# Moving the block sums of h to the head of a unit on GpSimd, tying ScalarE's copies of them to later matmuls, and making weight-block sums in three stages, in a fused attention and gated-MLP kernel

## The chip, the cores and the metric

The kernel runs on one core of a Trainium2 chip. Its time is the device time of one execution in microseconds (us); a set of runs is given by its median. In a profile the engines are PE (TensorE's matmuls; PEld is its weight loads), ACT (ScalarE), DVE (VectorE), POOL (GpSimd) and SP (SyncE, which here only issues DMA transfers). Each engine takes its own instructions in a fixed order and waits, one instruction at a time, for semaphores of the others.

## The reference, cut to what matters

All tensors are float32; S = 2048 rows, D = 576 columns, 32 heads of 18, F = 4608.

```python
x  = A_x
xn = layernorm(x)
q, k, v = split_heads(xn @ A_wqkv)            # 32 heads
s  = (softmax(q @ k.T * 18**-0.5) @ v) @ A_wo
gate, up = xn @ B_W_gate, xn @ B_W_up
h  = gate * (gate > 0) * up                   # 2048 x 4608
g  = silu(h @ B_W_down)
out = x + s * g
```

The matrix products are made with operands split into a high and a low part (float32r), three products for one: high by high, high by low, low by high.

## The kernel before

**Units.** After the layer norm and the QKV products the work runs in 144 units, numbered k = 0 to 143: four groups of 512 rows (g) times 36 blocks of 128 features of F (f). A unit is 27 steps of the up product (`pg`: 9 chunks of the contraction, three products each). Each step issues two matmuls, one on each half of TensorE's rows. Into these steps attention is dealt: up to 8 score matmuls per half for the row maxima of the next pair of heads (`pm`, reduced by VectorE, `mx`, L269), and from unit 16 on 8 per half for the exponentials of the present pair (`psx`, ScalarE's `p`, L97). So a unit in the middle of the run has 43 steps, 16 reductions and 16 exponentials. Both kinds of score, and the down product's results (`py`), use the same five PSUM banks in turn (`psS`).

**After its steps** a unit makes h: ScalarE takes the gate through Relu (`h<-pg`), VectorE multiplies by up (L739). An odd unit then runs the matmuls of P by V (`po`); an even one runs the down product of the two units before it (`py`). So a pair of units is, in PE's order: odd unit's steps, `po`, even unit's steps, `py`.

**The down product** is plain for the first 36 units. From unit 36 on two blocks of h are combined with two blocks of W_down in 7 products in place of 8: it needs sums of quarters of h1 and h2, the blocks of an even and the following odd unit (`first_half`, `second_half`), and the matching sums of weight blocks, which units 1 to 35 make and store in DRAM (`wtd`; `make_items`, `make_step`). Each sum of h is made by GpSimd into a scratch tile (`hr`, in a single buffer of tag `e`), copied by ScalarE as its high part (`ha`, `hb`, `hd`, `hc`), and GpSimd subtracts the copy for the low part (`low`). The results of the 7 products are added up by VectorE and, by way of ScalarE's copies (`add`, L879), by GpSimd (`c`, `y`).

**What sets the order.** PE, GpSimd and VectorE take their instructions in the order in which the code issues them, and so does SP until unit 17. ScalarE's are placed by a scheduler unless they are pinned. `up_end` puts the functions that make the sums into `at_step`, keyed by the step of the next unit at which they run. In a unit GpSimd's program begins with `split_up(k + 1)`, which makes the high and low parts of the next unit's up weights (`gw<-rg`, a cast and a subtraction), then the rows of `run_later` (`nr`), then what the steps issue. In the odd units of the last pair of heads `out_weights` loads and splits a block of wo, ahead of the steps.

**Group ends.** When f is 35 the sums of the group are combined (`combine`, 8 additions for each of two halves), and a gate (`gate_step`: Tanh on ScalarE, two GpSimd operations, a store) runs at two steps of each of the next units. The x tiles of the next group of rows are loaded in the last unit of a group (`load_x`).

**Weight blocks.** `make_step` runs three times in most units below 16 and five times in a unit from 16 to 35. Each time it ends the item before (GpSimd's subtraction `ws`, the store to `wtd`) and starts the next: a sum `wt` on VectorE (below unit 16) or GpSimd, and ScalarE's copy `ws` (L965). Tiles `wt` and `ws` have two buffers each.

Of the kernel before, what the change touches and what calls it, by code (L numbers as in the profile page):

```python
# [12 lines left out]
ALU = mybir.AluOpType  # L13
# [6 lines left out]
def kernel(  # L20
# [43 lines left out]
    def pool(stack, name, bufs, side="left", **kw):  # L64
        return stack.enter_context(tc.tile_pool(name=name, bufs=bufs, side=side, reuse_waits="tile", **kw))

    def mm(*args, **kw):
        return tc.keep_in_program_order(nc.tensor.matmul(*args, **kw))  # L68

# [696 lines left out]
    def low(t, cs, raw):  # L766
        gp.tensor_tensor(t[:, 1, cs], raw, t[:, 0, cs].bitcast(F32), ALU.subtract)

    def first_half(h):

        s, z = slice(0, 256), slice(256, 512)
        st = {}

        def raws():
            a = st["a"] = hp.tile([P, 2, 512], F32R, tag="hh", name="ha", bufs=3)
            r = st["r"] = wl.tile([P, D], F32, tag="e", name="hr", bufs=1)
            nc.scalar.activation(a[:, 0, s], h[:, s], AF.Copy)
            gp.tensor_tensor(r[:, s], h[:, z], h[:, s], ALU.subtract)
            nc.scalar.activation(a[:, 0, z], r[:, s], AF.Copy)

        def lows():
            a, r = st["a"], st["r"]
            low(a, s, h[:, s])
            low(a, z, r[:, s])
            hops[2] = a, 0
            hops[5] = a, 2

        return {2: [raws], 8: [lows]}

    def second_half(hs):  # L790

        h1, h2 = hs
        s, z = slice(0, 256), slice(256, 512)
        st = {}

        def raws():
            b = st["b"] = hp.tile([P, 2, 512], F32R, tag="hh", name="hb", bufs=3)
            d = st["d"] = mw[0].tile([P, 2, 256], F32R, name="hd", bufs=1)
            r = st["r"] = wl.tile([P, D], F32, tag="e", name="hr", bufs=1)
            nc.scalar.activation(b[:, 0, z], h2[:, z], AF.Copy)  # L800
            gp.tensor_tensor(r[:, s], h2[:, s], h2[:, z], ALU.subtract)
            nc.scalar.activation(b[:, 0, s], r[:, s], AF.Copy)
            gp.tensor_tensor(r[:, z], h1[:, s], h2[:, z], ALU.add)
            nc.scalar.activation(d[:, 0], r[:, z], AF.Copy)

        def lows():
            b, d, r = st["b"], st["d"], st["r"]
            low(b, z, h2[:, z])
            low(b, s, r[:, s])
            low(d, s, r[:, z])  # L810
            hops[6] = b, 0
            hops[3] = b, 2
            hops[0] = d, 0
            c = st["c"] = hp.tile([P, 2, 512], F32R, tag="hh", name="hc", bufs=3)
            r = st["r"] = wl.tile([P, D], F32, tag="e", name="hr", bufs=1)
            gp.tensor_tensor(r[:, :512], h1, h2, ALU.add)
            nc.scalar.activation(c[:, 0], r[:, :512], AF.Copy)

        def rest():
            c, r = st["c"], st["r"]  # L820
            low(c, slice(0, 512), r[:, :512])
            hops[4] = c, 0
            hops[1] = c, 2

        return {2: [raws], 8: [lows], 13: [rest]}

# [17 lines left out]
    def down_made(k):  # L844
# [94 lines left out]
    def make_items(fp):  # L939
# [9 lines left out]
        def start(m, on):  # L949
# [7 lines left out]
            if op is not None:  # L957
# [5 lines left out]
                x0 = t  # L963
            s_ = pw.tile([P, 2, HC], F32R, name="ws")
            nc.scalar.activation(s_[:, 0], x0, AF.Copy)  # L965
            st[m] = x0, s_

# [4 lines left out]

        return [(load, start, end, m) for m in (None, 1, 4, 0, 2, 3, 5, 6)]

    for fp in range(NF // 2):
        items.extend(make_items(fp))
    open_items = []

    def make_step(on):
        while open_items:  # L980
            end, m = open_items.pop()
            end(m)
        if items:
            load, start, end, m = items.pop(0)
            if m is None:
                load()
            else:
                start(m, on)
                open_items.append((end, m))

# [53 lines left out]
    def gate_step(spill_=True):  # L1044
        if gates:
            y, t = gates.pop(0)
            e = wl.tile([P, D], F32, name="e", bufs=1)
            tc.keep_in_program_order(nc.scalar.activation(e, y, AF.Tanh, scale=0.5))
            gp.tensor_scalar(e, e, 0.5, 0.5, op0=ALU.mult, op1=ALU.add)
# [124 lines left out]

    def emit_unit(k, ex, ns, mx, nm):
        if k - 1 in rds:
            split_down(k - 1)
        steps = dict(at_step)
        at_step.clear()
        if k not in rds and k not in dws and k != NF - 1:  # L1180
# [9 lines left out]
        if k % 2:  # L1190
            if k in rds:
                split_down(k)
            for _ in range(2):
                if to_load:
                    out_weights(to_load.pop(0))
        n = KC * len(PRODUCTS) + ns + nm
# [204 lines left out]
```

## Time and profile before

| | |
|---|---|
| median of 3 runs | 3601.24 us (3600.57 to 3614.94) |
| the profiled execution | 3614.0 us |
| its span, first to last instruction | 3612.2 us |
| mean granted TensorE clock | 0.876 |
| busy: PE, PEld, DVE, ACT, POOL | 81%, 59%, 53%, 47%, 48% |

Times in the views are us from the span's start. A row of the timeline gives start, duration, engine, line, operation, tiles written and read, shape and count, and in brackets how long the engine sat idle before it and what ended that. A row of the waits says who waited for whom: us in total, times, longest. A row of the windows gives a stretch, its length, each engine's busy time (with the number of instructions), the granted TensorE clock (1.00 is full), the share of time for which the 16 DMA engines were busy, and GB/s. L68 and L85 are helpers through which all matmuls and all GpSimd instructions pass.

### The profile page before, as it was taken

The numbers are of one execution on the slowest core, as the hardware profiler recorded it, in microseconds if no ns is written. First come the engines' busy times: TensorE is split into PE (matmuls) and PEld (weight loads), VectorE is DVE, ScalarE is ACT, GpSimd is POOL, SyncE is SP. The second block draws the span as 40 slices with busy tenths as digits, with TensorE's granted clock in tenths as the row PEclk, the third lists the DMA queues.
The fourth block names the chain that finished last, engine by engine and source line by source line (L and its number), as shares of the span: only waits on it lengthen the run. The fifth ranks groups of instructions, "written<-read, shape, count | busy, mean of one in ns | idle before, by whom it ended". The sixth has DMA issues, their size and how long they took to land.

```text
span 3612.2 us, 63126 instructions
## 1 busy us (share of the span) xinstructions
PE 2920.0 (81%) x24653; PEld 2138.8 (59%) x24653; DVE 1898.3 (53%) x3118; ACT 1710.9 (47%) x3761; POOL 1737.2 (48%) x1762
## 2 busy tenths in 40 slices
PE   9957778777747888989855998888882889888789
PEld 8846665555435666666633666666652566666558
DVE  5234444555425666666633766666661666666215
ACT  3211124444424655555523655565552565566553
POOL 4235554555425444554424455445532645544556
PEclk9978888888868989998976999899985999999899
DMA  8543443433314332333313333333322333332227
GB/s 273 183 145 113 125 121 94 119 118 96 118 64 125 88 93 82 91 92 105 88 63 95 94 86 97 101 93 88 94 74 85 110 90 91 93 86 75 81 85 221
DMA packets 324977, 382.12 MB, mean 106 GB/s; under 512 B 33480, under 2 KB 214472, under 8 KB 324680
## 3 DMA queue, kind: packets, MB, share of 16 engines
q1 hardware_dynamic: 316936, 350.43, 33.3%
q0 software_dynamic: 7744, 27.66, 2.2%
q8 instruction: 195, 3.19, 0.4%
q14 instruction: 102, 0.84, 0.1%
HBM read 293.78 MB, written 83.69 MB: 104 GB/s over the span
## 4 chain that ended last, share of the span: by engine, by line
PE 31%; POOL 31%; DMA 9%; ACT 5%; issue 4%; SPq 1%; DVE 0%; ACTq 0%; POOLq 0%; DVEq 0%
PE pg L68 15%; POOL gw L85 12%; PE psx L68 6%; PE pm L68 5%; POOL hr L85 5%; POOL y L85 4%; POOL c L85 4%; DMA x<-xTd 3%; PE py L68 3%; ACT p L97 2%; DMA rg<-in_B_W_up_dram 2%; POOL hb L85 2%; PE pw L68 1%; SPq L97 1%; DMA wtd<-ws 1%
## 5 line engine op out<-in xcount | busy, mean ns | idle before, releaser
L269 DVE TENSOR_REDUCE mx<-pm 128x1 f32<-128x512 f32 x2048 | 1370.0, 689 | 1126.1 <-PE pm L68 923.4
L68 PE MATMUL pg<-x,gw 64*128 64x512 f32 x7533 | 1624.8, 439 | 86.4 <-DMA x<-xTd 72.7
L68 PEld LDWEIGHTS pg<-x,gw 64*128 64x128 f32 x7533 | 1135.5, 212 | 238.3 <-DMA x<-xTd 79.3
L97 ACT ACTIVATE p<-psx 128x512 f32<-128x512 f32 x2048 | 1098.3, 601 | 227.4 <-PE psx L68 163.6
L85 POOL CAST gw<-rg 128x1152 fp32r<-128x1152 f32 x131 | 151.1, 1153 | 659.1 <-PE pg L68 436.7
L68 PE MATMUL po<-p,va 128*32 128x512 f32 x4096 | 456.8, 598 | 0.0
L85 POOL TENSOR_TENSOR c<-add,c 128x288 f32<-128x288 f32 x204 | 157.9, 807 | 584.3 <-ACT add L879 584.3
L68 PE MATMUL psx<-qT,kq 56*128 56x512 f32 x608 | 263.7, 446 | 129.9 <-ACT p L97 129.9
L85 POOL TENSOR_TENSOR gw<-rg,gw 128x1152 fp32r<-128x1152 f32 x131 | 346.0, 2641 | 10.6
L68 PEld LDWEIGHTS po<-p,va 128*32 128x32 f32 x4096 | 126.7, 110 | 296.1 <-issue 285.2
L68 PE MATMUL psx<-kq,kA 56*128 56x512 f32 x512 | 224.5, 450 | 88.9 <-ACT p L97 88.9
L68 PE MATMUL psx<-kq 56*128 56x512 f32 x512 | 227.7, 459 | 84.4 <-ACT p L97 84.4
L68 PE MATMUL psx<-qT,kA 56*128 56x512 f32 x416 | 185.8, 461 | 119.3 <-ACT p L97 119.3
L68 PE MATMUL pm<-kq,qT 54*128 54x512 f32 x608 | 260.4, 453 | 17.8 <-ACT p L97 17.8
L68 PE MATMUL pm<-kq 54*128 54x512 f32 x512 | 213.8, 440 | 37.9 <-ACT p L97 24.3
L68 PE MATMUL pm<-kA,kq 54*128 54x512 f32 x512 | 220.2, 455 | 28.8 <-DMA kA<-kd 19.0
L68 PEld LDWEIGHTS psx<-qT,kq 56*128 56x128 f32 x608 | 128.4, 211 | 161.4 <-ACT p L97 146.2
L68 PE MATMUL pm<-kA,qT 54*128 54x512 f32 x416 | 172.1, 436 | 23.9 <-ACT p L97 23.9
L739 DVE TENSOR_TENSOR h<-pg,h 128x512 f32<-128x512 f32 x144 | 98.3, 683 | 159.5 <-ACT h L97 107.6
L965 ACT ACTIVATE ws<-wt 128x288 fp32r<-128x288 f32 x90 | 39.8, 443 | 298.6 <-DMA wtd<-ws 158.5
L68 PEld LDWEIGHTS psx<-kq 56*128 56x128 f32 x512 | 110.9, 217 | 114.7 <-ACT p L97 101.8
L68 PEld LDWEIGHTS psx<-kq,kA 56*128 56x128 f32 x512 | 109.0, 213 | 116.8 <-ACT p L97 104.1
(138 smaller groups left out, 4490.0 us busy)
## 6 DMA issues: line engine op xcount, KB each, us to landing
w<-wtd SPq DMA_DIRECT2D x378, 288.0 KB
rg<-in_B_W_gate_dram SPq DMA_DIRECT2D x131, 288.0 KB
rg<-in_B_W_up_dram SPq DMA_DIRECT2D x131, 288.0 KB
wtd<-ws SPq DMA_DIRECT2D x126, 288.0 KB
x<-xTd SPq DMA_DIRECT2D x36, 512.0 KB
rd<-in_B_W_down_dram SPq DMA_DIRECT2D x36, 288.0 KB
wp<-in_B_W_down_dram SPq DMA_DIRECT2D x36, 288.0 KB
qd<-hh POOLq DMA_DIRECT2D x16, 512.0 KB, 6.8
```

Source lines behind the costliest of these rows:

```text
L68: return tc.keep_in_program_order(nc.tensor.matmul(*args, **kw))
L85: return lambda *args, **kw: tc.keep_in_program_order(op(*args, **kw))
L97: i = op(*args, **kw)
L269: vec(nc.vector.tensor_reduce(mx[:, h, b, j, c : c + 1], ps, axis=AX.X, op=ALU.max))
L739: vec(nc.vector.tensor_tensor(h, ps[1], h, ALU.mult))
L965: nc.scalar.activation(s_[:, 0], x0, AF.Copy)
```

## The change

1. **Sums first.** The GpSimd sums of h (`raws`) run under key 0, at the very head of a unit, ahead of `split_up`; the sum of all of h1 and h2, made at step 8 before, joins them and is written over h1.
2. **Copies tied.** ScalarE's copies of the sums go through `copy_now`, which makes a copy wait for the newest matmul issued: in an odd unit at steps 11 and 13, in an even one at 7, 14, 15 and 17. The low parts move from steps 8 and 13 to 22, 23 and 27.
3. **Group ends.** `combine` runs whole at the head of a unit, behind the sums, where it ran at steps 11 and 21. Gates run at steps 24 and 33 (17 and 27 before), their Tanh tied to the newest matmul. `out_weights` runs at steps 25 and 29 of an odd unit, no longer at its head.
4. **Three stages.** `make_step` subtracts and stores the item started two calls ago, copies the one started at the last call (tied), and starts a new one without its copy.

The core of the diff:

```diff
+    def copy_now(dst, src):
+        after(nc.scalar.activation(dst, src, AF.Copy), newest[0])
...
-        return {2: [raws], 8: [lows]}
+        return {
+            0: [raws],
+            11: [lambda: copy_now(st["a"][:, 0, s], h[:, s])],
+            13: [lambda: copy_now(st["a"][:, 0, z], st["r"][:, s])],
+            22: [lows],
+        }
...
             gp.tensor_tensor(r[:, s], h2[:, s], h2[:, z], ALU.subtract)
-            nc.scalar.activation(b[:, 0, s], r[:, s], AF.Copy)
             gp.tensor_tensor(r[:, z], h1[:, s], h2[:, z], ALU.add)
-            nc.scalar.activation(d[:, 0], r[:, z], AF.Copy)
+            gp.tensor_tensor(h1, h1, h2, ALU.add)
...
-        return {2: [raws], 8: [lows], 13: [rest]}
+        return {
+            0: [raws],
+            7: [lambda: copy_now(st["b"][:, 0, z], h2[:, z])],
+            14: [lambda: copy_now(st["b"][:, 0, s], st["r"][:, s])],
+            15: [lambda: copy_now(st["d"][:, 0], st["r"][:, z])],
+            17: [lambda: copy_now(st["c"][:, 0], h1)],
+            23: [lows], 27: [rest],
+        }
...
-                at_step[11] = [lambda: run_tasks(todo[:1])]
-                at_step[21] = [lambda: run_tasks(todo[1:])]
+                at_step.setdefault(0, []).extend((lambda j=j: combine(j)) for j in range(2))
...
     def make_step(on):
-        while open_items:
-            end, m = open_items.pop()
-            end(m)
+        ended = open_items.pop(0)
+        if ended:
+            ended[1](ended[2])
+        if open_items[0]:
+            open_items[0][0](open_items[0][2])
+        open_items.append(None)
...
     def emit_unit(k, ex, ns, mx, nm):
+        steps = dict(at_step)
+        at_step.clear()
+        for fn in steps.pop(0, ()):
+            fn()
...
-            if i in (17, 27):
+            if k % 2 and i in (25, 29) and to_load:
+                out_weights(to_load.pop(0))
+            if i in (24, 33):
                 gate_step()
```

On GpSimd an even unit of the steady part begins, before the change, with the weight split (`gw`), and each sum (`hr`) stands next to its low parts. In these rows h_16842 is the even unit's block h1 and h_17154 the odd one's, h2:

```order
L85 CAST gw<-rg 128x1152
L85 TENSOR_TENSOR gw<-rg,gw 128x1152
L85 TENSOR_TENSOR hr<-h_17154 128x256
L85 TENSOR_TENSOR hr<-h_16842,h_17154 128x256
L85 TENSOR_TENSOR hb<-h_17154,hb 128x256
L85 TENSOR_TENSOR hb<-hr,hb 128x256
L85 TENSOR_TENSOR hd<-hr,hd 128x256
L85 TENSOR_TENSOR hr<-h_16842,h_17154 128x512
L85 TENSOR_TENSOR hc<-hr,hc 128x512
```

With the change the same unit (its blocks are h_16832 and h_17144 there) reads:

```order
L88 TENSOR_TENSOR hr<-h_17144 128x256
L88 TENSOR_TENSOR hr<-h_16832,h_17144 128x256
L88 TENSOR_TENSOR h_16832<-h_16832,h_17144 128x512
L88 CAST gw<-rg 128x1152
L88 TENSOR_TENSOR gw<-rg,gw 128x1152
L88 TENSOR_TENSOR hb<-h_17144,hb 128x256
L88 TENSOR_TENSOR hb<-hr,hb 128x256
L88 TENSOR_TENSOR hd<-hr,hd 128x256
L88 TENSOR_TENSOR hc<-h_16832,hc 128x512
```

The three sums have moved ahead of the split, and all low parts stand behind it.

On ScalarE, from the odd unit's second copy to the even unit's exponentials, the rows before are (`p` are exponentials, `h` the Relu):

```order
L97 ACTIVATE p<-psx 128x512
L779 ACTIVATE ha<-hr 128x256
L97 ACTIVATE p<-psx 128x512 x15
L97 ACTIVATE h_17154<-pg_16983 128x512
L800 ACTIVATE hb<-h_17154 128x256
L802 ACTIVATE hb<-hr 128x256
L804 ACTIVATE hd<-hr 128x256
L817 ACTIVATE hc<-hr 128x512
L97 ACTIVATE p<-psx 128x512 x16
```

and with the change:

```order
L773 ACTIVATE ha<-h_16832 128x256
L100 ACTIVATE p<-psx 128x512
L773 ACTIVATE ha<-hr 128x256
L100 ACTIVATE p<-psx 128x512 x10
L100 ACTIVATE h_17144<-pg_16976 128x512
L100 ACTIVATE p<-psx 128x512 x3
L773 ACTIVATE hb<-h_17144 128x256
L100 ACTIVATE p<-psx 128x512 x3
L773 ACTIVATE hb<-hr 128x256
L100 ACTIVATE p<-psx 128x512
L773 ACTIVATE hd<-hr 128x256
L773 ACTIVATE hc<-h_16832 128x512
```

The copies now stand among the exponentials: `ha<-hr` behind six of the unit's 16 (one before), `hb<-hr` behind six and `hc` behind seven (none before).

On ScalarE in unit 21, one of the odd units that make weight-block sums, the copies `ws` stand before the change behind 6, 9, 11 and 13 exponentials:

```order
L97 ACTIVATE p<-psx 128x512 x6
L965 ACTIVATE ws<-wt 128x288
L97 ACTIVATE p<-psx 128x512 x3
L965 ACTIVATE ws<-wt 128x288
L97 ACTIVATE p<-psx 128x512 x2
L965 ACTIVATE ws<-wp 128x288
L97 ACTIVATE p<-psx 128x512 x2
L965 ACTIVATE ws<-wp 128x288
```

and with it:

```order
L100 ACTIVATE p<-psx 128x512
L773 ACTIVATE ws<-wt 128x288
L100 ACTIVATE p<-psx 128x512 x8
L773 ACTIVATE ws<-wt 128x288
L100 ACTIVATE p<-psx 128x512
L773 ACTIVATE ws<-wt 128x288
L100 ACTIVATE p<-psx 128x512 x5
L773 ACTIVATE ws<-wp 128x288
```

The first copy is now that of a sum made in the unit before; the first one whose sum is made in this unit has moved from behind the sixth to behind the ninth exponential.

More of the change, by code (lines that the diff above doesn't have):

```diff
@@ L65, in pool @@
         return stack.enter_context(tc.tile_pool(name=name, bufs=bufs, side=side, reuse_waits="tile", **kw))
+    newest = [None]
     def mm(*args, **kw):
-        return tc.keep_in_program_order(nc.tensor.matmul(*args, **kw))
+        newest[0] = tc.keep_in_program_order(nc.tensor.matmul(*args, **kw))
+        return newest[0]
     def vec(i):
@@ L796, in raws @@
         def raws():
[L797 to L800, printed above, removed]
+            st["b"] = hp.tile([P, 2, 512], F32R, tag="hh", name="hb", bufs=3)
+            st["c"] = hp.tile([P, 2, 512], F32R, tag="hh", name="hc", bufs=3)
+            st["d"] = mw[0].tile([P, 2, 256], F32R, name="hd", bufs=1)
+            st["r"] = r = wl.tile([P, D], F32, tag="e", name="hr", bufs=1)
             gp.tensor_tensor(r[:, s], h2[:, s], h2[:, z], ALU.subtract)
-            nc.scalar.activation(b[:, 0, s], r[:, s], AF.Copy)
             gp.tensor_tensor(r[:, z], h1[:, s], h2[:, z], ALU.add)
-            nc.scalar.activation(d[:, 0], r[:, z], AF.Copy)
+            gp.tensor_tensor(h1, h1, h2, ALU.add)
         def lows():
@@ L813, in lows @@
             hops[0] = d, 0
[L814 to L817, printed above, removed]
         def rest():
-            c, r = st["c"], st["r"]
-            low(c, slice(0, 512), r[:, :512])
+            c = st["c"]
+            low(c, slice(0, 512), h1)
             hops[4] = c, 0
             hops[1] = c, 2
-        return {2: [raws], 8: [lows], 13: [rest]}
+        return {
[6 more added lines that the diff above has]
+        }
     made_w = {}
@@ L963, in start, with middle @@
                 x0 = t
-            s_ = pw.tile([P, 2, HC], F32R, name="ws")
-            nc.scalar.activation(s_[:, 0], x0, AF.Copy)
-            st[m] = x0, s_
+            st[m] = x0, pw.tile([P, 2, HC], F32R, name="ws")
+        def middle(m):
+            x0, s_ = st[m]
+            copy_now(s_[:, 0], x0)
         def end(m):
@@ L971, in end @@
             sp.dma_start(wtd[fp, m], s_.bitcast(F32))
-        return [(load, start, end, m) for m in (None, 1, 4, 0, 2, 3, 5, 6)]
+        return [(load, start, middle, end, m) for m in (None, 1, 4, 0, 2, 3, 5, 6)]
     for fp in range(NF // 2):
         items.extend(make_items(fp))
-    open_items = []
+    open_items = [None, None]
     def make_step(on):
-        while open_items:
-            end, m = open_items.pop()
-            end(m)
-        if items:
-            load, start, end, m = items.pop(0)
-            if m is None:
+        ended = open_items.pop(0)
[4 more added lines that the diff above has]
+        open_items.append(None)
+        if items:
+            load, start, middle, end, m = items.pop(0)
+            if m is not None:
+                start(m, on)
+                open_items[1] = middle, end, m
+            elif load not in loaded:
+                loaded.append(load)
                 load()
-            else:
-                start(m, on)
-                open_items.append((end, m))
+    loaded = []
     def down(k):
@@ L1047, in gate_step @@
             e = wl.tile([P, D], F32, name="e", bufs=1)
-            tc.keep_in_program_order(nc.scalar.activation(e, y, AF.Tanh, scale=0.5))
+            after(tc.keep_in_program_order(nc.scalar.activation(e, y, AF.Tanh, scale=0.5)), newest[0])
             gp.tensor_scalar(e, e, 0.5, 0.5, op0=ALU.mult, op1=ALU.add)
@@ L1192, in emit_unit @@
                 split_down(k)
-            for _ in range(2):
-                if to_load:
-                    out_weights(to_load.pop(0))
         n = KC * len(PRODUCTS) + ns + nm
@@ L1242, in emit_unit @@
             if k == NF:
-                while items or open_items:
+                while items or any(open_items):
                     make_step(nc.gpsimd)
```

8 lines of the change are left out of this document (2 added, 6 removed).

## Prediction

> **What bounds the kernel now.** The span splits by what PE does, so I read the waits first, for who holds PE up. Columns: who, on whom, us in total, times, longest.
>
> ```profile
> PE psx L68 <- ACT p L97: 422.5, 135, 42.4
> ...
> ACT ha L779 <- POOL hr L85: 233.8, 54, 13.3
> ACT hb L802 <- POOL hr L85: 211.0, 54, 45.7
> ...
> ACT hc L817 <- POOL hr L85: 163.2, 54, 3.0
> ```
>
> PE waits for exponentials, and ScalarE waits, 54 times for each of three copies, once in each pair of units from 36 on, for a GpSimd sum. While a copy waits, the exponentials behind it wait too, and their PSUM banks stay full. The timeline of one pair shows both sides, ScalarE first:
>
> ```profile
> 1252.72 0.42 ACT L800 ACTIVATE hb<-h 128x256 fp32r<-128x256 f32 x1 [1.66 <-DVE h L739]
> 1255.55 0.42 ACT L802 ACTIVATE hb<-hr 128x256 fp32r<-128x256 f32 x1 [2.41 <-POOL hr L85]
> ...
> 1259.68 0.63 ACT L817 ACTIVATE hc<-hr 128x512 fp32r<-128x512 f32 x1 [3.02 <-POOL hr L85]
> ...
> 1266.99 3.87 ACT L97 ACTIVATE p<-psx 128x512 f32<-128x512 f32 x7 [0.19 <-PE psx L68]
> ...
> 1283.36 0.42 ACT L779 ACTIVATE ha<-hr 128x256 fp32r<-128x256 f32 x1 [4.25 <-POOL hr L85]
> ```
>
> and GpSimd over the same stretch:
>
> ```profile
> 1251.69 2.65 POOL L85 TENSOR_TENSOR gw<-rg,gw 128x1152 fp32r<-128x1152 f32 x1
> ...
> 1254.78 0.73 POOL L85 TENSOR_TENSOR hr<-h 128x256 f32<-128x256 f32 x1
> ...
> 1258.36 1.29 POOL L85 TENSOR_TENSOR hr<-h,h 128x512 f32<-128x512 f32 x1
> ...
> 1276.50 2.35 POOL L85 TENSOR_TENSOR y<-add,y 128x288 f32<-128x288 f32 x3
> 1278.78 1.15 POOL L85 CAST gw<-rg 128x1152 fp32r<-128x1152 f32 x1
> 1280.02 2.63 POOL L85 TENSOR_TENSOR gw<-rg,gw 128x1152 fp32r<-128x1152 f32 x1
> 1282.59 0.73 POOL L85 TENSOR_TENSOR hr<-h 128x256 f32<-128x256 f32 x1
> ```
>
> In the odd unit (from 1277.84) the sum stands behind a weight split of 1.15 + 2.63 us, and `ha` waits 4.25 us for it. In the even one `hc` waits 3.02 us for the sum at 1258.36, which five low parts and sums precede. What that costs PE is in the windows: first three undisturbed stretches between units 37 and 134 with all engines, then the same three for line 817 alone, whose count is the number of pairs.
>
> ```profile
> 1103.25:1824.95 721.70, 645.98 (x5455) 454.14 (x5453) 462.43 (x749) 425.14 (x923) 367.46 (x376) 0.91 0.34 95
> 1995.43:2671.35 675.92, 605.97 (x5122) 427.01 (x5121) 433.57 (x705) 400.83 (x873) 336.27 (x347) 0.92 0.33 93
> 2835.61:3340.32 504.71, 453.14 (x3842) 318.32 (x3841) 324.99 (x529) 300.65 (x655) 250.88 (x259) 0.92 0.32 91
> ```
>
> ```profile
> 1103.25:1824.95 721.70, 10.71 (x17) 0.91 0.34 95
> 1995.43:2671.35 675.92, 10.08 (x16) 0.92 0.33 93
> 2835.61:3340.32 504.71, 7.57 (x12) 0.92 0.32 91
> ```
>
> 45 pairs take 1902.33 us, 42.27 each. Single segments follow (first busy column PE, third DVE, fourth ACT): an odd unit's steps, an even unit's twice, an odd unit's without any stall, then `po` and `py`.
>
> ```profile
> 1277.84:1294.61 16.77, 13.30 (x91) 9.93 (x87) 9.81 (x17) 9.28 (x19) 6.82 (x8) 0.80 0.58 166
> 1301.61:1312.98 11.37, 10.68 (x92) 8.38 (x88) 9.13 (x14) 8.94 (x18) 3.05 (x3) 1.00 0.18 39
> 1257.52:1271.19 13.67, 12.22 (x91) 9.50 (x89) 9.16 (x14) 9.75 (x19) 3.31 (x4) 0.88 0.14 31
> 1155.49:1166.25 10.76, 10.76 (x90) 8.40 (x86) 9.78 (x17) 9.38 (x18) 0.10 (x1) 1.00 0.83 252
> 1294.61:1301.61 7.00, 7.00 (x66) 1.97 (x65) 4.78 (x8) 1.78 (x4) 6.92 (x7) 1.00 0.29 73
> 1271.19:1277.84 6.65, 6.65 (x86) 5.88 (x84) 4.50 (x9) 4.75 (x16) 4.39 (x6) 1.00 0.07 23
> ```
>
> The odd unit loses twice: PE is idle for 3.47 us (16.77 less 13.30), and the clock falls to 0.80. The even one has a gap of 0.69 us at full clock or of 1.45 us at 0.88. So the bound is not an engine but a queue order: a copy at the wrong place on ScalarE, and the clock that PE loses through the gap.
>
> **The change, part by part.**
>
> *Odd units.* The sum comes first: GpSimd's additions end at 1278.85 (1276.50 + 2.35), the sum of 0.73 us would end at 1279.6. A step takes 10.76 / 43 = 0.25 us, so the copy tied to step 13 is released at 1277.84 + 3.3 = 1281.1, 1.5 us after its sum is there. ScalarE doesn't wait for GpSimd, and nothing is held. The split moves 0.73 us back, to about 1283.4; what it makes is wanted by the next unit, 10.76 + 7.00 us after this one's start. The low parts follow at once and are read a whole unit later. What is left is the row without a stall: 10.76 us, where VectorE is busy for 9.78 us and is late next.
>
> *Even units.* Three sums (0.73 + 0.73 + 1.29 = 2.75 us) go ahead of the split. h is ready when the first copy was, 1252.72, so they end near 1255.5, during `po`; the steps start at 1257.52, and the copies are tied to steps 7 to 17 (1.8 to 4.3 us later). No copy waits. The split (1.15 + 2.65 us) then ends near 1259.3, no longer at 1254.3, and is wanted by the next unit, 11 + 6.65 us after 1257.52. The waits for the ties cost nothing where ScalarE has run out of exponentials; but four copies now stand among 16 exponentials, three of them between steps 14 and 17. An exponential takes 3.87 / 7 = 0.55 us, the copies 3 x 0.42 + 0.63 = 1.89 us: 10.7 us with the exponentials, and the Relu besides, against 10.76 us of steps. Bounds: 10.76 us, if the banks cover it, and 11.37 us, today's row with a gap of 0.69 us. I take 11.1, nearer to 11.37, since three copies and two exponentials in four steps (1.0 us) make about a microsecond of arrears.
>
> *A pair* is then 10.76 + 7.00 + 11.1 + 6.65 = 35.51 us, 6.76 less; times 45 is **304 us**. Should the even unit stay at 10.76 it is 319.
>
> *Last pair of heads.* Odd units there have 35 steps. The three with a long gap, and one without (the first two also split wo ahead of the sums):
>
> ```profile
> 3388.10:3411.97 23.87, 11.29 (x74) 8.61 (x71) 0.85 (x3) 8.86 (x18) 10.87 (x11) 0.71 0.45 137
> 3436.13:3457.95 21.82, 9.90 (x74) 7.46 (x70) 0.85 (x3) 8.52 (x18) 10.85 (x11) 0.77 0.49 149
> 3482.36:3497.20 14.84, 11.35 (x75) 8.56 (x71) 0.85 (x3) 8.85 (x18) 6.76 (x7) 0.77 0.61 179
> 3521.12:3531.06 9.94, 9.65 (x74) 6.69 (x70) 1.83 (x5) 8.18 (x19) 3.11 (x5) 1.00 0.77 236
> ```
>
> ```profile
> 3399.73 0.66 POOL L85 CAST kq<-rd 128x576 fp32r<-128x576 f32 x1 [4.75 <-DMA rd<-in_A_wo_dram]
> ```
>
> 60.53 less 3 x 9.94 is 31 us. But the two wo blocks, moved to steps 25 and 29, still share one buffer: GpSimd waits again some 4.75 us for each, now ahead of the next even unit's sums. SP, which issues those loads, waits with them; its weight loads have a unit of slack. That costs nothing if the copies' steps cover it and 4.75 us if nothing does; I charge 2.5 us to each of two even units and count **26 us**.
>
> *Units 16 to 35.* Five weight-block steps a unit. One odd unit, GpSimd, then ScalarE, then the stretch of nine pairs with all engines:
>
> ```profile
> 798.24 0.79 POOL L85 TENSOR_TENSOR wt<-wp 128x288 f32<-128x288 f32 x1
> ```
>
> ```profile
> 799.06 0.44 ACT L965 ACTIVATE ws<-wt 128x288 fp32r<-128x288 f32 x1 [7.82 <-POOL wt L85]
> ...
> 801.50 0.44 ACT L965 ACTIVATE ws<-wt 128x288 fp32r<-128x288 f32 x1 [0.54 <-DMA wtd<-ws]
> ```
>
> ```profile
> 517.46:994.04 476.58, 360.09 (x2991) 258.38 (x2990) 241.31 (x387) 217.40 (x463) 247.25 (x244) 0.86 0.36 111
> ```
>
> The sum `wt` stands behind three weight splits of GpSimd that this change leaves ahead of it, so it still ends near 799.0. Its copy comes three exponentials later on ScalarE, and PE stops some 6 steps (1.5 us) later. But the next copy then waits for a store whose subtraction comes only after that sum, near 799.8; today the copy at 801.50 waits for a store whose subtraction had ended by 798.24, 3.3 us earlier. I expect most of the gap back. Bounds: at the floor (9 x 35 us = 315) it would gain 160 us; a longer second wait would lose some 3 us in each of ten odd units. I take **15 us**, near the lower end, because the releasing row doesn't move; I allow -25 to +60. Below unit 16 VectorE makes the sums:
>
> ```profile
> DVE wt L960 <- POOL ws L85: 36.9, 7, 6.1
> ```
>
> A sum there now waits for a subtraction that GpSimd is given at the same step (one step earlier before), with the reductions queued behind it; the copies, in turn, wait less. Between all of these 36.9 us gone and as much again added, PE feeling less than half: 0 +- 15 us.
>
> *Group ends.* In unit 72 ScalarE's wait of 42 us goes, since the sums no longer stand behind a split whose weights are late. PE only, with what released it:
>
> ```profile
> 1902.01 0.79 PE L68 MATMUL psx<-qT,kq 56*128 56x512 f32 x1 [42.37 <-ACT p L97]
> ...
> 1934.23 1.22 PE L68 MATMUL pg<-x,gw 64*128 64x512 f32 x4 [8.51 <-DMA x<-xTd]
> ```
>
> But the last x tile comes at 1934 either way: the loads follow each other from unit 71 on, and PE would wait for them instead. Nothing is gained at these three places. `combine` has the same 16 additions; they now hold the split and the low parts back instead of the first gate. 0 +- 5 us at each of two.
>
> *Sum.* 304 + 26 + 15 = 345 us. The profiled execution took 3614.0 us, so 3269; it lies 12.8 us above the median of the runs, 3601.24, so the median should be **3256 us**.
>
> **The rivals.** *ScalarE takes GpSimd's place.* The even unit's copies set it back so far that PE waits 1.45 us and loses clock, as in the row of 13.67 us. A pair is then 38.08 us, 189 us gained, 230 with the rest: 3371. For: ScalarE's 10.7 us; against: `po` and `py` leave it idle for 5 and 2 us to catch up. [...]
>
> *The clock does not come back.* Stretches at 0.91 to 0.92 might be so for another reason than gaps. Then only the idle goes: (721.70 - 645.98) + (675.92 - 605.97) + (504.71 - 453.14) = 197 us, 28 us of the last units' gaps and 15: 240 us, 3361. Against: every quoted segment without a gap over 0.7 us stands at 1.00.
>
> *Slower: lockstep.* Each of six copies in a pair holds ScalarE until its matmul has run, while PE waits for banks that the exponentials behind the copy would free. If each stopped PE as long as that 1.45 us gap, 2.9 us with the clock (13.67 less 10.76), a pair would gain 6 x 2.9 = 17.4 us over 35.5 and be 10.6 us slower than today: 45 times, 478 us, about 4040 with the rest. It decides from 6.76 / 6 = 1.1 us per copy. Against: a tie is behind the exponentials of earlier steps, so it can last a step or two, 0.25 to 0.5 us.
>
> *The stall only moves.* The sums come early but something in the weight-block part or at group ends takes the 345 us: 0 +- 0.5%. Nothing in the rows is that large.
>
> **How the numbers follow.** Forecast 0.76, ScalarE 0.09, clock 0.08, lockstep 0.03, moved 0.02, a mixture beyond the range 0.02. The forecast's own bounds: 10.76 in the even units and +60 in the middle part, 319 + 31 + 60 = 410 us, 3191; downward, 11.37 us (-12), -25 instead of 15 (-40) and -25 below unit 16 and at group ends, 268 us, 3333. The next case takes it to 3371: the range is 3190 to 3375. Half a per cent is about what a measurement of this kernel can tell from no change: faster 0.95, same 0.02, slower 0.03.
>
> **What would show it.** Right: the waits of `ha`, `hb` and `hc` on `hr` gone from 608 us to under 50; the three stretches at 35 to 36 us a pair with a clock of 0.97 or more; odd units' steps near 10.8 us; units 72 and 108 as long as now; units 16 to 35 hardly changed. Wrong: copies waiting for PE with idle PE beside them, a clock at 0.91 without gaps, or ScalarE waiting for `wt` for longer than now.

## The result and the profile after

The kernel after takes **3234.83 us** (median of 3 runs, 3232.67 to 3239.11), the kernel before 3601.24: a ratio of 0.8974, 95% interval 0.8938 to 0.9009. The forecast was 3256. The profiled execution's span is 3237.3 us, 374.9 less than before, at a mean clock of 0.914 (0.876 before).

The chain that ended last, by engine, on the page of the kernel before and then on that of the kernel after:

```profile
PE 31%; POOL 31%; DMA 9%; ACT 5%; issue 4%; SPq 1%; DVE 0%; ACTq 0%; POOLq 0%; DVEq 0%
...
PE 54%; DMA 10%; POOL 7%; ACT 4%; issue 3%; SPq 1%; DVE 0%; POOLq 0%; ACTq 0%; DVEq 0%
```

The waits of ScalarE (who, on whom: us in total, times, longest):

```profile
ACT ws L773 <- DMA wtd<-ws: 228.9, 49, 19.0
...
ACT e L1066 <- POOL ha L88: 29.1, 3, 13.4
...
ACT hb L773 <- POOL hr L88: 5.2, 2, 3.3
...
ACT hc L773 <- POOL h L88: 0.9, 2, 0.4
...
ACT hd L773 <- POOL hr L88: 0.5, 2, 0.3
```

The 608 us for which `ha`, `hb` and `hc` waited for GpSimd's sums are down to 6.1 (`hb` 5.2, `hc` 0.9); `ha` has no row left. The timeline of an odd unit shows why, GpSimd and then ScalarE:

```profile
1154.81 2.33 POOL L88 TENSOR_TENSOR y<-add,y 128x288 f32<-128x288 f32 x3
1157.22 0.74 POOL L88 TENSOR_TENSOR hr<-h 128x256 f32<-128x256 f32 x1
1157.91 1.14 POOL L88 CAST gw<-rg 128x1152 fp32r<-128x1152 f32 x1
```

```profile
1156.82 3.02 ACT L100 ACTIVATE p<-psx 128x512 f32<-128x512 f32 x5 [0.59 <-PE psx L70]
1159.73 0.41 ACT L773 ACTIVATE ha<-h 128x256 fp32r<-128x256 f32 x1
1160.04 0.59 ACT L100 ACTIVATE p<-psx 128x512 f32<-128x512 f32 x1
1160.52 0.42 ACT L773 ACTIVATE ha<-hr 128x256 fp32r<-128x256 f32 x1
```

The sum ends at 1157.96 and its copy starts 2.6 us later, behind six exponentials and without a wait; before, it stood behind one and waited 4.25 us. The windows, for stretches of 17, 16 and 12 pairs of units, with all engines (PE first, clock third from the end):

```profile
1073.35:1675.94 602.59, 597.05 (x5456) 421.28 (x5454) 452.29 (x749) 409.25 (x922) 370.89 (x377) 1.00 0.41 114
1846.39:2408.59 562.20, 559.69 (x5123) 394.41 (x5122) 424.25 (x704) 386.37 (x873) 341.39 (x349) 1.00 0.41 112
2574.14:2995.90 421.76, 419.85 (x3842) 295.52 (x3841) 318.22 (x528) 289.74 (x655) 255.38 (x261) 1.00 0.40 109
```

The 45 pairs take 1586.55 us, 35.26 each, at full clock; the last 28, clear of the transition out of unit 36, take 35.14. Single segments, an odd unit's steps and an even one's:

```profile
1156.16:1166.82 10.66, 10.66 (x90) 8.05 (x87) 9.44 (x17) 9.44 (x20) 6.88 (x7) 1.00 0.46 138
1173.82:1184.61 10.79, 10.67 (x92) 8.56 (x89) 9.06 (x14) 9.56 (x20) 5.44 (x5) 1.00 0.30 64
```

And the stretches that answer to the other terms: after, units 17 to 34 (from the end of unit 16's steps to the end of unit 34's), a group end (units 71 to 74), and the last units; then the last two of before:

```profile
512.66:963.03 450.37, 350.83 (x2989) 261.21 (x2987) 240.66 (x387) 215.63 (x463) 248.20 (x244) 0.86 0.40 119
1675.94:1846.39 170.45, 87.08 (x642) 59.78 (x639) 53.85 (x89) 52.10 (x113) 62.50 (x69) 0.69 0.24 78
2995.90:3179.33 183.43, 168.71 (x1528) 120.22 (x1524) 50.42 (x95) 116.24 (x280) 117.13 (x121) 0.96 0.43 124
```

```profile
1824.95:1995.43 170.48, 86.25 (x642) 59.11 (x640) 54.31 (x89) 52.15 (x114) 64.69 (x71) 0.70 0.25 79
3340.32:3554.20 213.88, 175.19 (x1528) 122.30 (x1524) 51.54 (x95) 118.06 (x280) 115.94 (x121) 0.91 0.36 106
```

With the other boundaries read in the same way, the two spans differ so:

| stretch | gained, us | forecast |
|---|---|---|
| to the end of unit 16's steps | 4.8 | 0 |
| units 17 to 34 | 26.2 | 15 |
| units 35 and 36 | -1.1 | 0 |
| 45 pairs | 315.8 | 304 |
| both later group ends | 0.0 and -1.3 | 0 |
| unit 135 to the end of the units | 30.5 | 26 |
| tail | 0.0 | 0 |
| sum | 374.9 | 345 |

### The profile page after: what moved, and what is told of

Its sections match the earlier page's. It is cut to its first block, busy times and chain, and to the rows that moved or that the text cites. A ratio compares the mean times of both kernels' runs of the same rounds, so it can differ in the third digit from the quotient of the medians.

```text
span 3237.3 us, 63467 instructions
## 1 busy us (share of the span) xinstructions
PE 2772.1 (86%) x24653; PEld 2047.1 (63%) x24653; DVE 1867.7 (58%) x3118; ACT 1665.0 (51%) x3761; POOL 1746.8 (54%) x1762
## 4 chain that ended last, share of the span: by engine, by line
PE 54%; DMA 10%; POOL 7%; ACT 4%; issue 3%; SPq 1%; DVE 0%; POOLq 0%; ACTq 0%; DVEq 0%
PE pg L70 17%; PE po L70 11%; PE py L70 11%; PE pm L70 7%; PE psx L70 6%; DMA x<-xTd 6%; DMA wtd<-ws 2%; POOL gw L88 2%; PE pw L70 2%; POOL y L88 2%; ACT p L100 1%; SPq L100 1%; DMA rg<-in_B_W_up_dram 1%; ACT hc L773 1%; ACT hd L773 1%
## 5 line engine op out<-in xcount | busy, mean ns | idle before, releaser
L272 DVE TENSOR_REDUCE mx<-pm 128x1 f32<-128x512 f32 x2048 | 1345.0, 687 | 790.4 <-PE pm L70 647.3
L70 PE MATMUL pg<-x,gw 64*128 64x512 f32 x7533 | 1495.0, 410 | 171.8 <-DMA x<-xTd 153.4
L70 PEld LDWEIGHTS pg<-x,gw 64*128 64x128 f32 x7533 | 1062.0, 195 | 302.8 <-DMA x<-xTd 165.9
L70 PE MATMUL psx<-qT,kq 56*128 56x512 f32 x608 | 231.9, 410 | 33.9 <-ACT p L100 32.2
L70 PE MATMUL pm<-kq,qT 54*128 54x512 f32 x608 | 240.3, 417 | 19.1 <-ACT p L100 19.1
L70 PE MATMUL psx<-kq 56*128 56x512 f32 x512 | 199.7, 414 | 49.1 <-ACT p L100 47.6
L88 POOL TENSOR_TENSOR hr<-h 128x256 f32<-128x256 f32 x108 | 79.4, 735 | 289.7 <-DVE nm L1099 151.0
L70 PE MATMUL psx<-kq,kA 56*128 56x512 f32 x512 | 193.5, 406 | 20.5 <-ACT p L100 19.1
L890 ACT ACTIVATE add<-py 128x288 f32<-128x288 f32 x357 | 141.3, 411 | 61.2 <-PE py L70 26.5
L70 PE MATMUL py<-dw,hh 64*128 64x288 f32 x1728 | 145.6, 327 | 25.9 <-DVE mx L272 12.9
```

The source lines that it names most:

```text
L70: newest[0] = tc.keep_in_program_order(nc.tensor.matmul(*args, **kw))
L88: return lambda *args, **kw: tc.keep_in_program_order(op(*args, **kw))
L272: vec(nc.vector.tensor_reduce(mx[:, h, b, j, c : c + 1], ps, axis=AX.X, op=ALU.max))
L890: pinned(nc.scalar.activation(src, outs_[p][j], AF.Copy))
```

## The experiments

The theory: a copy on ScalarE that is early, of a sum on GpSimd that is late, holds the exponentials; PE stops when its banks are full; and a long stop costs the clock as well. The rivals: one part of the change does it all; the clock has another cause; the middle part or the group ends hide something of the gain or the loss. All kernels but the first profile's are the kernel after with an edit. The kernel before, run beside each, had medians of 3608.7 to 3610.3 us, so ratios are compared; 0.001 is 3.6 us.

**Sums first, copies not tied.**

```diff
-            11: [lambda: copy_now(st["a"][:, 0, s], h[:, s])],
-            13: [lambda: copy_now(st["a"][:, 0, z], st["r"][:, s])],
...
+            nc.scalar.activation(st["a"][:, 0, s], h[:, s], AF.Copy)
+            nc.scalar.activation(st["a"][:, 0, z], r[:, s], AF.Copy)
```

> The kernel after, but its six copies are issued without ties, right behind their sums: on ScalarE four stand ahead of the even unit's exponentials and two ahead of the odd unit's, as before the change; the GpSimd sums stay at the head of the unit. Theory (the loss was the wait for a late sum): the sums end 1.5 to 2 us before or after the steps begin, so a copy waits about 1.3 us at the most, which today's PSUM banks cover in most pairs; a pair stays at 35.1 to 36 us and the time at 3235 to 3280 us. Rival (the copies' place among the exponentials is what counts): the pair goes back to 40 us or more, the clock in the steady stretches to about 0.92, and the time to 3450 to 3600 us.

3246.73 us, 0.8997 (0.8983 to 0.9012). The windows of an even and an odd unit's steps, and ScalarE's largest wait for a sum:

```profile
1169.45:1179.56 10.11, 10.11 (x90) 8.54 (x88) 9.08 (x14) 8.62 (x16) 5.39 (x5) 1.00 0.31 68
1186.22:1197.83 11.61, 10.40 (x91) 8.15 (x87) 9.89 (x17) 9.09 (x19) 6.89 (x7) 1.00 0.63 173
```

```profile
ACT ha L785 <- POOL hr L88: 90.6, 51, 2.5
```

Time and pair are those of the theory, not quite its way there: the copy waits 1.8 us (90.6 / 51) and not 1.3, and the banks don't cover it. PE stops for 1.21 us (11.61 less 10.40), but the clock stays at 1.00. The ties are worth 1 us in the odd unit, and they *cost* 0.68 us in the even one, which without them takes 10.11 and not 10.79.

**Ties, but late sums.**

```diff
-        for fn in steps.pop(0, ()):
-            fn()
         if k - 1 in rds:
             split_down(k - 1)
...
+        for fn in steps.pop(0, ()):
+            fn()
         n = KC * len(PRODUCTS) + ns + nm
```

> The kernel after with its ties, but the functions of key 0 (sums, combine) run behind the weight split again. Theory: in the odd unit the sum ends near 1283.4 on the scale of the first profile, 2.3 us after the copy is released at step 13; that copy holds the exponentials behind it, PE stops for some 1 to 2 us and loses clock on top, so odd units' steps take 12.5 to 14 us in place of 10.65; in the even unit the sums still come before the ties and its 10.8 us stay. 45 pairs by 2 to 3.3 us: 3325 to 3385 us. Rival (the ties alone are enough, since a tied copy stands behind a few exponentials): 3235 to 3250 us, odd steps below 11 us.

3287.31 us, 0.9112 (0.9093 to 0.9130): neither number. An even and an odd unit:

```profile
1170.82:1181.62 10.80, 10.70 (x91) 8.69 (x89) 9.05 (x14) 9.56 (x20) 3.46 (x4) 1.00 0.16 36
1188.27:1200.11 11.84, 10.66 (x90) 7.96 (x86) 9.44 (x17) 9.53 (x20) 6.91 (x8) 1.00 0.72 206
```

```profile
ACT ha L773 <- POOL hr L88: 57.0, 50, 3.3
```

PE does stop, but for 1.18 us, and the clock does not fall. The copy has its turn only behind six exponentials, later than its tie lets it go (the sixth ends at 1192.74 here; step 13 comes near 1191.6, by 0.25 us a step), and waits 1.14 us (57.0 / 50), not 2.3. The theory's price was wrong twice: it reckoned the wait from the tie, and it added the clock to every stop.

**Neither.** Both edits together; three stages and the rest stay.

> The kernel after with both of its steady-state parts undone, the ties (as in the run without ties) and the place of the sums (as in the run with late sums); three stages, gates and wo's blocks stay as changed. Theory (either part alone keeps PE's stop short enough for the banks and the clock, and only without both is the copy so early and its sum so late that PE stops for 3.5 us and the clock falls): odd steps go back to 16 to 17 us as in the first profile, even steps stay at 10 to 11 us since their sums end before the steps begin, a pair is 40 to 41.5 us, 45 pairs cost 220 to 290 us: 3455 to 3525 us. Rival (the two parts add up, 8 us and 49 us in the runs above): 3290 to 3300 us.

3477.79 us, 0.9640 (0.9626 to 0.9654). An even and an odd unit, then the waits:

```profile
1223.36:1233.48 10.12, 10.12 (x90) 8.55 (x88) 9.11 (x14) 9.47 (x18) 3.38 (x5) 1.00 0.21 44
1240.15:1257.09 16.94, 13.49 (x91) 9.95 (x87) 9.85 (x17) 9.38 (x19) 6.83 (x8) 0.80 0.54 163
```

```profile
ACT ha L785 <- POOL hr L88: 225.5, 54, 5.4
```

The odd unit is the first profile's again: 3.45 us of stop and a clock of 0.80. The four kernels side by side, with the mean of the 44 pairs in units 39 to 70, 75 to 106 and 111 to 134:

| | pair, us | ratio |
|---|---|---|
| neither | 39.9 | 0.9640 |
| sums first alone | 35.3 | 0.8997 |
| ties alone | 36.2 | 0.9112 |
| both (after) | 35.1 | 0.8974 |

From "neither", the first part alone gives 0.0643, the second alone 0.0528, and both 0.0666. They are two cures of one fault in the odd unit; either takes the stop in the rows above from 3.45 us to about 1.2 (1.21 and 1.18), and the clock there from 0.80 to 1.00.

The even unit was cured by something else. "Neither" still makes the sum of all of h1 and h2 together with the other sums, ahead of the low parts, and the low parts at their later steps. Its even unit takes 10.12 us where the kernel before took 11.37 or 13.67, and `hc` waits 0.94 us a time (50.9 / 54) and no longer 3.0:

```profile
ACT hc L816 <- POOL h L88: 50.9, 54, 1.0
```

The same 44 pairs took 42.2 us each in the kernel before. So 2.3 of the 7.1 us gained were there already in "neither"; no run takes this part away by itself.

**A scale of late sums.** The odd unit's sum is repeated.

```diff
-            gp.tensor_tensor(r[:, s], h[:, z], h[:, s], ALU.subtract)
+            for _ in range(1 + dose()):
+                gp.tensor_tensor(r[:, s], h[:, z], h[:, s], ALU.subtract)
```

> The kernel after, but in the odd units the sum for the tied copy is made 1 + n times over, n running through 0, 4, 0, 5, 0, 6, 0, 7, 0, 8, 0, 10 from pair to pair, so that one run holds a scale of delays. A sum takes 0.73 us and the copy is released 1.5 us behind the first one, so it comes 1.4, 2.1, 2.9, 3.6, 4.3 and 5.8 us late for n = 4, 5, 6, 7, 8, 10. Theory (a late copy holds the exponentials, PE stops when the banks are full, and the clock falls if the stop is long): with the 1.1 us that the banks covered in the run with late sums (2.3 us late, gap 1.18) the gaps are 0.3, 1.0, 1.8, 2.5, 3.2 and 4.7 us, and the steps 10.65 us plus the gap up to some 1.3 us of gap; from somewhere between 1.2 us (no fall in the run with late sums) and 3.5 us (fall in the first profile) on, another 1.7 us for 3.4 us at half clock. Rival (the clock fell in the first profile for another reason): steps are 10.65 us plus the gap all along, 15.4 us at n = 10.

One run, 3317.29 us. PE's gap in the odd unit, its steps, and PE's time at half clock in them, one unit of each kind:

```
extra sums   0      4      5      6      7      8      10
gap, us      0      0.70   1.49   2.29   3.10   3.90   5.50
steps, us    10.66  11.38  12.18  14.54  15.33  16.12  18.34
at half, us  0      0      0      3.41   3.41   3.41   4.71
```

In this run the gap grew by 0.80 us a sum, and half clock came on top from about 2.3 us, with two of four such gaps in the steady stretches. The rival would have 10.66 + 5.50 = 16.2 us at the end, not 18.34: the clock falls because of the gap.

**A finer scale**, to settle why the same gap sometimes costs the clock. The extra sums are cut to steps of 64 columns.

> The kernel after, with the odd unit's sum made late by eleven delays in turn, chosen for gaps of about 0.8 to 2.8 us on PE. In the records of the clock all changes lie on one grid of 3.413 us. Theory (the clock of a window is set by the window before it: a window in which PE is idle for more than some 1.4 to 1.5 us gives one at half clock): a gap below 1.4 us never brings a half clock, one above 2.9 us always, one between does where 1.5 us of it or more fall into one window; sorted by the idle time of the window before, windows at half and at full clock separate, but for a narrow band. Rival (the length of the gap alone decides, at about 2.3 us, where of four gaps two brought a fall): they separate by length of the gap, and not by window.

One run, 3379.24 us. Windows of the grid around a gap of 2.06 us, then around one of 2.86 us:

```profile
2056.05:2059.46 3.41, 1.35 (x12) 1.07 (x12) 0.97 (x3) 2.10 (x5) 3.25 (x4) 1.00 0.13 49
2059.46:2062.87 3.41, 3.41 (x18) 2.88 (x17) 1.98 (x4) 2.18 (x5) 3.00 (x3) 0.50 0.04 10
2172.10:2175.51 3.41, 2.21 (x20) 1.60 (x16) 2.24 (x4) 1.31 (x3) 3.10 (x5) 1.00 0.79 261
2175.51:2178.93 3.42, 1.77 (x16) 1.50 (x18) 1.23 (x2) 2.64 (x6) 3.26 (x4) 1.00 0.02 5
2178.93:2182.34 3.41, 3.41 (x31) 2.68 (x27) 2.83 (x6) 3.10 (x7) 2.50 (x3) 1.00 0.15 41
```

The shorter gap lies whole in one window (PE busy for 1.35 of 3.41) and the next window stands at 0.50. The longer one is cut into 1.2 and 1.65 us, and the clock stays at 1.00. In the first steady stretch of this run the windows at full clock that were followed by half clock had 1.87 us of idle or more, the others 1.73 or less; sorted by length of the gap the two do not separate.

Behind a window that is itself at half clock less idle time went with half clock. Here PE is idle for 2.21 us in the first window and for only 0.64 us, the rest of the same gap, in the second, and yet the third stays at half clock:

```profile
1236.85:1240.26 3.41, 1.20 (x12) 0.70 (x8) 1.29 (x2) 0.62 (x2) 3.10 (x6) 1.00 0.44 167
1240.26:1243.67 3.41, 2.77 (x14) 2.21 (x16) 1.38 (x2) 2.65 (x6) 3.33 (x2) 0.50 0.00 0
1243.67:1247.09 3.42, 3.42 (x20) 2.68 (x18) 1.39 (x2) 1.86 (x4) 1.43 (x3) 0.50 0.51 121
```

**Two stages again.** `make_step` as before the change.

```diff
+            nc.scalar.activation(st[m][1][:, 0], x0, AF.Copy)
...
-        ended = open_items.pop(0)
-        if ended:
-            ended[1](ended[2])
...
+        while open_items:
+            end, m = open_items.pop()
+            end(m)
```

> The kernel after with weight-block sums in two stages as before: a call ends the item before and starts the next with its copy at once. Theory by the two traces: units 16 to 34 took 476.6 us before and 450.4 us after, the units below 16 some 5 us less, and nothing else that runs there was changed, so three stages are worth 25 to 35 us: 3260 to 3270 us. Rival by the prediction's own value (15 us): 3250 us. Rival (worth nothing, the difference is the two traces' own): 3235 us.

3266.54 us, 0.9053 (0.9038 to 0.9068): 28 us, as the traces had it. Units 17 to 34 take 475.2 us there (518.66 to 993.84), as before the change (476.6).

**Three buffers for `ws`.**

```diff
-            st[m] = x0, pw.tile([P, 2, HC], F32R, name="ws")
+            st[m] = x0, pw.tile([P, 2, HC], F32R, name="ws", bufs=3)
```

> The kernel after with three buffers in place of two for the tile (ws) that the weight-block copies fill and the stores empty. Theory for units 16 to 35 (the copies wait for a store, 228.9 us in 49 waits, since the stores stand behind other transfers on SP, and the exponentials behind the copies wait with them): a third buffer gives each store one more call, 2 us, so some 100 us of these waits go, and about half of the gap in units 16 to 35: 20 to 50 us gained, 3185 to 3215 us. Rival (the GpSimd sums behind three splits hold the copies, as the prediction had it for these units): 3230 to 3240 us.

3188.75 us, 0.8835 (0.8822 to 0.8848): 50 us. ScalarE's waits in the kernel before, for the stores and for GpSimd's sums; the same two here; then units 17 to 34:

```profile
ACT ws L965 <- DMA wtd<-ws: 168.6, 42, 19.0
...
ACT ws L965 <- POOL wt L85: 110.1, 41, 7.8
```

```profile
ACT ws L773 <- DMA wtd<-ws: 96.6, 23, 18.8
ACT ws L773 <- POOL wt L88: 60.2, 10, 7.9
```

```profile
493.60:914.77 421.17, 343.04 (x2991) 257.29 (x2989) 238.73 (x387) 211.93 (x462) 246.13 (x242) 0.88 0.42 126
```

29 us are gained there and 19 us ahead of them. The kernel after had no wait for GpSimd's `wt`; three stages had turned it into more waiting for the stores (228.9 us). The stores bound these units; with a third buffer the late sums show at once, with 60.2 us, so both causes that the prediction named were there, one behind the other.

**Group ends and wo as before.** `combine` at steps 11 and 21, wo's blocks at the head of the odd unit.

```diff
-                at_step.setdefault(0, []).extend((lambda j=j: combine(j)) for j in range(2))
+                at_step.setdefault(11, []).append(lambda: run_tasks(todo[:1]))
+                at_step.setdefault(21, []).insert(0, lambda: run_tasks(todo[1:]))
...
```

> The kernel after with the combination of a group's sums back at steps 11 and 21, and wo's blocks back at the head of the odd unit, there ahead of the sum. Theory by the two traces: the wo blocks cost the odd units 28.9 us before (23.87 + 21.82 - 2 x 8.42) and cost the even units after about 5.6 + 4.6 us and the down products behind them 3 + 1.5 us; so putting them back costs about 14 us; units 73 and 109 are as long in both traces, so the combination's place is worth nothing: 3245 to 3252 us. Rival (the combination at the head delays the split and the gates, which is the gap of 13.4 us in units 73 and 109): 13 to 26 us come back there, and the time is 3220 to 3238 us.

3236.73 us, 0.8970 (0.8956 to 0.8983): no difference that can be measured. The odd units with wo take 17.48 and 18.55 us and no longer 8.42, 19.2 us more; the even ones and the down products behind them take 14.6 us less. So moving wo gave 5 us there and not the theory's 14 (units 135 to 142 take 149.97 us here and 144.95 in the kernel after). They don't show in the total, since this profile is 6 us shorter ahead of unit 35, where the two kernels don't differ. The time lies in the rival's range, but not for the rival's reason: the gap in units 73 and 109 is 13.29 and 13.32 us here, 13.37 and 13.31 in the kernel after. The combination's place is worth nothing.

**x tiles in two transfers.**

```diff
-                xc.rearrange("p a s -> p (a s)").bitcast(F32),
-                xTd[g, c // 2, c % 2 * R : c % 2 * R + R].unsqueeze(0).to_broadcast([2, R, 1024]),
...
+                    xc[t * R : (t + 1) * R].rearrange("p a s -> p (a s)").bitcast(F32),
+                    xTd[g, c // 2, c % 2 * R : c % 2 * R + R],
```

> The kernel after, but each x tile is loaded by two transfers, one for each half of the partitions, in place of one that repeats its rows for both halves. The rows and results are the same. Theory (units 36, 72 and 108 wait for x tiles, nine of them one after the other at 10 us each and 51 GB/s, because the one transfer runs on two of the 16 DMA engines): the tiles come in a few us each as the other loads do, the steps of units 72 and 108 fall from 87 and 89 us to 15 to 30 us, and the time by 150 to 200 us: 3035 to 3085 us. Rival (the rate is that of the source or the queue, or something else binds right behind, as VectorE and the weights do): less than 60 us gained, 3175 us or more.

**2987.23 us**, 0.8279 (0.8263 to 0.8296): 250 us, more than expected. Unit 72's steps in the kernel after, with 8 us of them, in which x tiles are all that is issued; then the same steps here, the down product behind them, and the next odd unit's steps:

```profile
1700.28:1787.09 86.81, 21.02 (x90) 13.18 (x88) 9.18 (x14) 11.69 (x22) 7.42 (x8) 0.53 0.18 61
...
1744.00:1752.00 8.00, 0.81 (x4) 0.09 (x2) 1.38 (x2) 0.60 (x1) 6.69 (x8) 0.50 0.14 55
```

```profile
1581.81:1592.59 10.78, 10.68 (x91) 8.71 (x88) 9.06 (x14) 10.16 (x21) 0.96 (x1) 1.00 0.89 201
1592.59:1614.40 21.81, 10.96 (x86) 10.06 (x84) 4.47 (x9) 4.46 (x15) 11.17 (x14) 0.61 0.42 118
1614.40:1640.96 26.56, 13.21 (x90) 10.43 (x87) 10.06 (x18) 11.14 (x22) 23.86 (x27) 0.75 0.37 112
```

The DMA engines' mean share goes from 0.18 to 0.89. Each of the three group ends gives 66 to 68 us (from unit 71's steps to unit 74's down product it is 103.1 us in place of 171.0). Some 50 us come from ahead of unit 16, where nothing was expected: the first down product starts at 222.55 us and no longer at 272.98, since the first group's tiles, and key loads queued behind them, had held PE in the kernel after for waits that are gone here:

```profile
PE pm L70 <- DMA kA<-kd: 18.9, 1, 18.9
PE po L70 <- DMA x<-xTd: 17.7, 2, 9.9
```

Two things are left at a group end. The down product in the second row takes 21.81 us, 8 more than in the kernel after (13.76), and waits for the low part of `hd` (5.03 us) and for weight sums (4.82), so a part of the stop has only moved. And the odd unit in the last row has its gates' Tanh wait on ScalarE 13.4 us for low parts that stand on GpSimd behind the combination.

The theory's two engines agree with the kernel after's trace: in those 8 us it has two packets in flight at once for 7.16 us, and a share of 0.14 of 16 engines is 2.2 engines' worth.

**Copies off the exponentials.** The even unit's four untied at its head; the odd unit's two behind its steps, with their low parts and gates; wo's blocks in a free buffer.

```diff
-            11: [lambda: copy_now(st["a"][:, 0, s], h[:, s])],
-            13: [lambda: copy_now(st["a"][:, 0, z], st["r"][:, s])],
-            22: [lows],
-        }
+        return {0: [raws], "end": [copies, lows]}
...
```

> The kernel after with its copies moved off the exponentials: the even unit's four are untied at its head (they ran so in the run without ties, where its steps took 10.12 us), and the odd unit's two, with their low parts, come behind its steps, while PE runs the products by V and ScalarE is idle for 5 of 7 us. For that the gates of odd units come behind the steps too, and wo's blocks are loaded into a buffer of their own, one for each odd unit. Theory (a copy among the exponentials costs PE small stalls, 0.5 to 0.66 us a unit, even without a visible gap): odd steps fall to about 10.15 us as well, a pair to 33.9 us, 54 us gained in 45 pairs and some 10 to 15 in the last units: 3165 to 3180 us. Rival (the odd unit's 10.65 us are set by VectorE, which enters it with the down product's last additions): the odd steps stay at 10.6 us: 3190 to 3200 us. Rival (GpSimd, busy for 6.9 of the 7 us, makes the even unit's sums late): a gap in the even unit, 3230 us or more.

3170.32 us, 0.8781 (0.8768 to 0.8794): 69 us. An even and an odd unit:

```profile
1170.33:1180.45 10.12, 10.12 (x91) 8.72 (x88) 9.10 (x14) 8.61 (x16) 5.32 (x5) 1.00 0.32 68
1187.11:1197.51 10.40, 10.40 (x90) 8.25 (x86) 9.44 (x17) 9.04 (x18) 5.49 (x5) 1.00 0.58 154
```

The odd unit lies between theory (10.15) and rival (10.6); why it keeps 0.28 us more than the even one stays open. The even one keeps 10.12 (10.79 in the kernel after), so copies among exponentials do cost PE here, without a gap that shows. The time is in the theory's range, in part by luck: the 45 pairs give 37 us and not 54, the last units 21 and not 10 to 15, two group ends 7, and 4.5 us lie ahead of unit 17, where this edit changes nothing.

**All three together.**

> The x tiles in two transfers, three buffers for ws, and the copies off the exponentials with wo's blocks apart, all three in one kernel. Theory (they act in different places: units 35, 36, 72 and 108; units 16 to 35; the 45 pairs and the last units): the ratios to the kernel before add up, 0.8974 - 0.0695 - 0.0139 - 0.0193 = 0.795: 2860 to 2875 us. Rival (what one frees another takes, as in units 73 and 109, where the combination's 13 us on GpSimd now come last): 2890 us or more.

**2883.24 us**, 0.7992 (0.7979 to 0.8005): 20% below the kernel before, 11% below the kernel after, and 15 us short of the sum of the three, between the theory's range and the rival's. By the profiles' spans 19 us are missing. 9 of them are ahead of unit 17, where the x tiles alone gave 49 us, the third buffer alone 19, and both together 64 (the 4.5 us of the third kernel there are not its edit's); 4 are in units 71 to 74. The 45 pairs and the last units give what they gave alone.

## Why the prediction was right, point by point

- **The bound** was read rightly: a copy early on ScalarE, its sum late on GpSimd, and the clock on top. "Neither" against "both" shows it for the odd units, 39.9 against 35.1 us a pair.
- **Odd units**: forecast 10.76, measured 10.66. The row without a stall was a good floor for this order of ScalarE, though not for the unit: without the copies among the exponentials it takes 10.40. The profile before had two such rows as well, 10.41 us at 2002.94 and 10.40 at 2842.95.
- **Even units** were mis-sized: forecast 11.1 us, measured 10.79. That is 14 us in 45 pairs, and the odd units' 0.1 us another 5; the 45 pairs gave only 12 us beyond 304, because the stretch behind unit 36 takes 7 us more than its pairs at 35.10 would. The arrears of "about a microsecond" were there as 0.67 us (10.79 less 10.12), but on a floor of 10.12 and not of 10.76: the row of 10.76 was an odd unit's.
- **What the parts do**: the working credited each copy's tie and each sum's place together and gave no price for one without the other. The runs show the two as nearly interchangeable in the odd unit. In the even unit the ties only cost; 2.3 us a pair came from the third sum's place ahead of the low parts and the low parts' later steps.
- **Last pair of heads**: 26 us forecast, 24.6 measured (30.5 less 5.8 for unit 135, 16.46 to 10.66), from two wrong terms. The odd units without a stall take 8.42 us, not the 9.94 of the row used; and wo's blocks cost 14.6 us, not 2 x 2.5. GpSimd's rows in unit 138 show it:

```profile
3052.56 0.67 POOL L88 CAST kq<-rd 128x576 fp32r<-128x576 f32 x1 [8.63 <-DMA rd<-in_A_wo_dram]
...
3057.64 0.66 POOL L88 CAST kq<-rd 128x576 fp32r<-128x576 f32 x1 [2.91 <-DMA rd<-in_A_wo_dram]
```

- **Units 16 to 35**: 15 forecast, 26.2 measured in units 17 to 34, inside the -25 to +60 allowed, and by the way forecast: the wait for the sum went (110.1 us), the wait for the store grew (168.6 to 228.9). Up to the end of unit 16's steps: 4.8 us, inside 0 +- 15. Kernels that differ in nothing there spread as widely (unit 17 starts between 514.25 and 519.06 us), so this says little.
- **Group ends**: nothing gained, as forecast, and for the reason given: with x tiles in two transfers the 87 us are 10.8. Unit 72's steps even grew, from 81.07 to 86.81 us, by what unit 71's lost (16.42 to 10.66), since PE waits in both kernels for the last x tile.
- **The median**: 3256 forecast, 3234.83 measured. The gains were 30 us larger than the sum; 8.5 of them don't show in the median, by luck, since the profile before lay 12.8 us above its median and the profile after 4.3 above its own.
- **Rivals.** ScalarE in GpSimd's place: no; the tied copies cost 0.67 us, not 2.9. The clock that does not come back: no, 1.00 in all three stretches. Lockstep: no; copies off the exponentials gained 0.91 us a pair, 0.15 a copy, against a point of decision of 1.1 us a copy. The stall only moves: no, no other stretch lost more than 1.3 us.

## What to carry to other kernels

On an engine that works in order, look for an instruction whose input is made late on another engine, and price it by the stop that it causes *beyond* what the buffers cover: either moving the producer up or the consumer down may be enough, and their gains need not add (here 0.0643 and 0.0528 of the ratio alone, 0.0666 together). A floor must come from a row of the same kind of unit. A wait that looks hidden behind a slow load is worth asking after the load itself: here two transfers in place of one broadcast were worth 250 us, two thirds of what the change gave.

## What the runs showed of the hardware

In the profiles before and after, the granted clock has two values, 1.00 and 0.50. Its records change 229 times before and 93 times after, and all these changes lie on a grid of 3.413 us, to within 2 ns. Counted is PE's idle time (gaps over 0.15 us) in each window of that grid, in units 17 to 134, against the clock of the next window:

| windows | next at 0.50: number, PE idle | next at 1.00: number, PE idle |
|---|---|---|
| before, at 1.00 | 92, 1.42 to 3.41 us | 519, 0 to 1.68 us |
| after, at 1.00 | 27, 1.64 to 3.41 us | 578, 0 to 1.58 us |
| before, at 0.50 | 122, 0.46 to 3.41 us | 92, 0 to 0.45 us |
| after, at 0.50 | 94, 0.57 to 3.41 us | 27, 0 to 0.24 us |

Between 1.42 and 1.68 us it went both ways in the kernel before (25 windows with half clock behind them, 16 with full), for a reason that stays open.

What a stop cost on top of itself was read in the two scales. In the first, steps behind gaps of 2.29 and 2.30 us that lie in one window took 14.54 and 14.52 us, and steps behind gaps of 2.31 and 2.33 us that the grid cuts 12.97 and 12.99, 1.55 us less. Gaps of 3.0 us or more had half clock behind them every time in both. In the finer one, steps with gaps of 2.86 and 2.99 us that reached 0.5 us or more into the window at half clock took 16.35 and 16.33 us, and others with gaps of the same length 15.10 and 15.22.
